# One change to a convolution and mixture-of-experts kernel: output stores of four evictions, other landing times in the list that orders the engines, and two GpSimd steps moved into that list

## The chip, the cores and the metric

The kernel runs on one core of a Trainium2 chip. The metric is the time of one execution on the device in microseconds (us). Three runs of the kernel before took 307.57, 302.77 and 307.64 us; their median is 307.57. The engines are TensorE (PE, with its weight loads as PEld), VectorE (DVE), ScalarE (ACT), GpSimd (POOL) and SyncE (SP), which issues all transfers (DMA) here.

## The reference

```python
def _attn_ref(x, weight_gen):            # x [8, 3584, 192], weight_gen [8, 3584, 8 heads, 7 taps]
    w = softmax(weight_gen, axis=-1)     # per position and head, 1e-9 added to the sum
    x_pad = concat([zeros(6 rows), x])   # causal: position s sees x[s-6 .. s]
    return einsum('bshk,bskhg->bshg', w, unfolded(x_pad))      # 24 channels per head

def _moe_ref(x, phi, w1, w2):            # x [28672, 192], phi [192, 32 slots]
    logits = x @ phi
    d = softmax(logits, axis=0)          # over all 28672 tokens, 1e-9 added to the sum
    slot_input = (d.T @ x).reshape(8 experts, 4 slots, 192)
    slot_out[e] = relu(slot_input[e] @ w1[e]) @ w2[e]          # 192 -> 1024 -> 192
    c = softmax(logits, axis=1)          # over the 32 slots
    return c @ slot_out
```

A position-dependent causal convolution of 7 taps feeds a mixture of experts, whose dispatch weights are normalised over all tokens. So nothing of the output can be computed before the last token has been convolved.

## The kernel before

**Tiles.** The 8 sequences are cut into 1,104 blocks of 26 positions; four blocks make a group (276 groups), two groups a pair (138), four pairs a block of the program's order (35, the last of two pairs), eight pairs a unit of the softmax over tokens (17, and a last one of two pairs). A chunk of taps serves eight groups, that is one block of the order; there are 35 chunks, the last one half as long.

**Stage 1, convolution (to about 221 us).** For each chunk the taps are loaded (`loadw`, L160) and pass through `tap_top` (DVE, the maximum over the taps, L171), `tap_sub` (POOL, L175), `tap_exp` (ACT, L179), `tap_sum` (three POOL steps, L188 to L190, or one on DVE), `tap_inv` (DVE, a reciprocal, L194), `tap_mul` (POOL, which writes the weights on the diagonals of `wide`, L202) and `tap_turn` (DVE, a transposition into one of three `band` buffers, L206). `taps` has three buffers too, `wide` only one. `conv` (PE, L230) multiplies bands with the rows of x, which `loadx` (L156) brings into five places of `big`; ACT copies the result to `tm` (L236); PE transposes it (L250), ACT copies that to `cm` (L257). In every second block follow, for the unit before, the scores (`logits`, PE, L281), their maximum (`top`, DVE, `mx` and `mq`, L288 and L290), a small product that gathers the maxima (`newmax`, PE, L306, and `nm`, DVE, L310), the exponentials `dd` (ACT, L318), their transposition `dt` (DVE, L327) and, one block on, the weighted sum (`dispatch`, PE, L346), which DVE adds to `accS` (L354).

**What sets the order.** In stage 1 each step is entered in a list by `op(engine, cost, reads, writes, function, ..., late, due)`. `late` is what passes after the step until its result can be used; the loads alone have one of some size. `model` goes through the list with these costs, keeps the entered order of PE and SP, picks for DVE, ACT and POOL the step with the least slack among those that can start, and yields a start for each step; the steps are written out in the order of these starts (L685). On the chip each engine runs its instructions strictly in that order and waits where an operand is missing. The numbers of the list aren't used on the chip in any other way.

**Stage 2, the experts (to about 244 us).** It is written by hand. `selO4` lies in the memory of `phi_sb`, which the scores read, and `si` in that of `fold`, which the POOL sums of the taps use; so both can be written only when those are done with. Two PE products pick the accumulators by even and odd slots (`pst`, L704 to L706), DVE copies them into the zeroed `si` (L707), `hidden` (L742) and `outputs` (L763) are the two layers. The weights `w2` are loaded into places of `big` that x no longer needs; `pace` and `mark` (L412) make each of these loads wait for a tiny POOL copy.

**Stage 3, the output (to the end).** Each piece of the output is two PE results of up to 468 columns in two PSUM banks (`rows`, L818), an eviction into `big` (`leave`, L823: DVE for each third one, from the second on, and ACT for the others) and a store (`store`, L830). `big` serves as a ring of 16 evictions. An item (0, h) is the first 128 channels of step h of 16, an item (1, h) the last 64 channels of two steps; each has two evictions, but the first one has three. Between the evictions stand the softmax steps over the slots for later steps of the output (`soft`, L85 to L99) and the transpositions `cT` (`turn`, L404).

## Time and profile before

| | |
|---|---|
| median of three runs | 307.57 us (302.77 to 307.64) |
| profiled execution | 305.91 us, span of its instructions 304.1 us |
| mean granted TensorE clock | 0.954 |
| busy PE, DVE, ACT, POOL | 263.5, 197.2, 189.6, 146.6 us |
| loads of taps | 34 of 182 KB and one of 91 KB |
| output stores | 27, of which 18 of 884 KB, 4 of 936 KB, 3 of 468 KB, 2 of 234 KB |
| written to memory | 22.04 MB |

The profile is that of one execution. A line such as "DVE top L171 <- DMA taps<-wh" says which engine waited at which line of the kernel, and for what; "in total, times, longest" follow. The chain of waits goes back from the last instruction, at each step to what released it. In lists of instructions in order of time the first number is the start after the span's begin and the second how long the piece lasted, both in us. In a table by stretches of time the columns are the length, then the busy time (and instructions) of PE, PEld, DVE, ACT and POOL, the granted TensorE clock, the busy share of the DMA engines and GB/s.

### The profile page before, as it was taken

The numbers are of one execution on the slowest core, as the hardware profiler recorded it, in microseconds if no ns is written. First come the engines' busy times: TensorE is split into PE (matmuls) and PEld (weight loads), VectorE is DVE, ScalarE is ACT, GpSimd is POOL, SyncE is SP. The second block draws the span as 40 slices with busy tenths as digits, with TensorE's granted clock in tenths as the row PEclk, the third lists the DMA queues.
The fourth block names the chain that finished last, engine by engine and source line by source line (L and its number), as shares of the span: only waits on it lengthen the run. The fifth ranks groups of instructions, "written<-read, shape, count | busy, mean of one in ns | idle before, by whom it ended". The sixth has DMA issues, their size and how long they took to land.

```text
span 304.1 us, 15222 instructions
## 1 busy us (share of the span) xinstructions
PE 263.5 (87%) x6646; PEld 213.7 (70%) x6646; DVE 197.2 (65%) x337; ACT 189.6 (62%) x399; POOL 146.6 (48%) x254
## 2 busy tenths in 40 slices
PE   8898998999999999999999999499899887889100
PEld 8787977888897888888988889488678632233000
DVE  8867757975787867775776855554056579995200
ACT  9896676576686767677767667255521268788400
POOL 8856556746468384665565463410017526550000
PEclk9999999999999999999999999979999999779855
DMA  6768676667677667666677666626748059999994
GB/s 184 220 180 240 201 214 199 208 205 207 185 216 202 201 187 202 195 194 193 185 222 216 188 204 195 195 81 182 255 130 314 3 202 416 421 410 417 419 418 204
DMA packets 26993, 69.24 MB, mean 228 GB/s; under 512 B 5936, under 2 KB 10800, under 8 KB 26928
## 3 DMA queue, kind: packets, MB, share of 16 engines
q1 hardware_dynamic: 26928, 68.28, 69.0%
q8 instruction: 52, 0.85, 1.2%
q14 instruction: 13, 0.11, 0.1%
HBM read 46.21 MB, written 22.04 MB: 224 GB/s over the span
## 4 chain that ended last, share of the span: by engine, by line
PE 69%; DMA 9%; DVE 7%; issue 4%; ACT 3%; POOL 3%; ACTq 1%; POOLq 0%; DVEq 0%
PE cv L230 30%; PE pt L250 14%; PE acb L346 7%; PE ls L281 7%; DMA out<-big 4%; DMA taps<-wh 4%; PE po L818 3%; PE so L763 2%; PE hpb L742 2%; PE acb L306 2%; DVE big L823 1%; DVE band L206 1%; POOL taps L175 1%; ACT big L823 1%; DVE cT L404 1%
## 5 line engine op out<-in xcount | busy, mean ns | idle before, releaser
L230 PE MATMUL cv<-big,band 128*26 128x96 f32 x4416 | 112.3, 250 | 3.6 <-issue 2.6
L230 PEld LDWEIGHTS cv<-big,band 128*26 128x26 f32 x4416 | 101.5, 130 | 13.0 <-issue 8.1
L236 ACT COPY tm<-cv 128x384 f32<-128x384 f32 x138 | 66.4, 482 | 57.6 <-PE cv L230 57.4
L206 DVE STREAM_TRANSPOSE band<-wide 128x1664 f32<-128x1664 f32 (+1 forms) x37 | 65.5, 1773 | 7.8 <-POOL wide L202 7.6
L250 PE MATMUL pt<-ident,tm 122*128 122x122 f32 x414 | 50.9, 272 | 0.2 <-issue 0.2
L257 ACT COPY cm<-pt 128x416 f32<-128x416 f32 x103 | 48.1, 511 | 1.9 <-PE pt L250 0.9
L250 PEld LDWEIGHTS pt<-ident,tm 122*128 122x128 f32 x414 | 44.5, 144 | 2.6 <-issue 0.4
L202 POOL TENSOR_TENSOR wide<-exps,sum 128x364 f32<-128x364 f32 (+1 forms) x36 | 28.5, 792 | 26.5 <-DVE sum L194 18.9
L175 POOL TENSOR_TENSOR taps<-taps,top 128x364 f32<-128x364 f32 (+1 forms) x36 | 28.5, 793 | 24.3 <-DVE top L171 24.0
L818 PE MATMUL po<-cT,so 32*128 32x442 f32 (+3 forms) x256 | 33.6, 629 | 5.4 <-ACT big L823 3.4
L823 ACT COPY big<-po 128x884 f32<-128x884 f32 (+2 forms) x33 | 28.1, 893 | 7.8 <-PE po L818 6.0
L818 PEld LDWEIGHTS po<-cT,so 32*128 32x128 f32 (+1 forms) x256 | 12.1, 171 | 26.4 <-ACT big L823 18.0
L188 POOL TENSOR_TENSOR si<-exps 128x208 f32<-128x208 f32 x32 | 20.3, 635 | 21.0 <-ACT exps L179 20.6
L281 PE MATMUL ls<-cm,phi_sb 128*32 128x208 f32 x544 | 28.9, 338 | 1.5 <-issue 1.5
L171 DVE TENSOR_REDUCE top<-taps 128x52 f32<-128x364 f32 (+1 forms) x37 | 17.7, 486 | 18.4 <-DMA taps<-wh 17.7
L346 PE MATMUL acb<-tm,dt 128*32 128x193 f32 x544 | 27.5, 328 | 2.3 <-issue 1.6
L87 POOL TENSOR_TENSOR LT<-LT,rm 128x544 f32<-128x544 f32 (+1 forms) x16 | 17.9, 1120 | 16.8 <-DVE rm L85 16.8
L288 DVE TENSOR_REDUCE mx<-ls 128x1 f32<-128x416 f32 x17 | 9.9, 584 | 24.0 <-PE ls L281 24.0
L281 PEld LDWEIGHTS ls<-cm,phi_sb 128*32 128x32 f32 x544 | 17.8, 109 | 6.9 <-issue 2.7
L346 PEld LDWEIGHTS acb<-tm,dt 128*32 128x32 f32 x544 | 18.0, 110 | 6.5 <-issue 3.1
L179 ACT ACTIVATE exps<-taps 128x364 f32<-128x364 f32 (+1 forms) x37 | 17.9, 493 | 6.3 <-POOL taps L175 6.3
L99 POOL TENSOR_TENSOR LT<-LT,sm 128x544 f32<-128x544 f32 (+1 forms) x16 | 17.9, 1121 | 6.8 <-DVE sm L97 6.6
(113 smaller groups left out, 260.1 us busy)
## 6 DMA issues: line engine op xcount, KB each, us to landing
big<-xh SPq DMA_DIRECT2D x276, 96.0 KB, 3.3
out<-big SPq DMA_DIRECT2D x18, 884.0 KB, 10.5
taps<-wh SPq DMA_DIRECT2D x34, 182.0 KB, 3.7
big<-w SPq DMA_DIRECT2D x8, 768.0 KB, 4.3
w1a_sb<-w1a SPq DMA_DIRECT2D x16, 256.0 KB, 3.6
out<-big SPq DMA_DIRECT2D x4, 936.0 KB, 4.9
w1b_sb<-w1b SPq DMA_DIRECT2D x8, 256.0 KB, 3.6
out<-big SPq DMA_DIRECT2D x3, 468.0 KB, 3.0
```

The source lines that it names most:

```text
L175: eng.tensor_tensor(out=t, in0=t, in1=each(tops.pop((c, b.start)), b.stop - b.start), op=ALU.subtract)
L188: eng.tensor_tensor(out=s, in0=t[:, :, :, 0:4], in1=t[:, :, :, 4:8], op=ALU.add)
L202: eng.tensor_tensor(out=dst, in0=exps[c % NEX][:, b, :, 0:KT], in1=each(m, n), op=ALU.mult)
L206: V.transpose(bands[c % NBAND][:, b].rearrange("p b j l -> p (b j l)"), wide[:, b].rearrange("p b j -> p (b j)"))
L230: P.matmul(cv[32 * blk : 32 * blk + T, o : o + 4 * GW], bands[g // 8 % NBAND][:, g // 4 % CH, :, i], xbd[:, place(t), :, b * GW : (b + 1) ...
L236: copy(tms[u % NTM][:, pr, 1 : 2 * D + 1], cvs[p % NCV][:, 0 : 2 * D])
L250: P.transpose(pt[:, at, 0:TR], tms[u % NTM][0:TR, pr, 1 + 128 * i : 129 + 128 * i], ident[0:TR, 0:TR])
L257: copy(cms[u].rearrange("p a i b j -> p (a i b) j")[:, at : at + n], pts.pop((k, j)).rearrange("p i (b j) -> p (i b) j", j=32)[:, 0:n, 0:T])
L281: P.matmul(lp[32 * blk : 32 * blk + 32, lo:hi, par, 0:T], phi_sb[:, 2 * par + i, :], cm[:, lo:hi, 1 if i else 2 * par, blk, :], start=(i = ...
L346: P.matmul(ac[32 * q : 32 * q + 32], dt[:, g, :], tm[:, g // 2, o : o + D + 1], start=(g < 4), stop=(g + 4 >= 2 * n))
L818: P.matmul(po[dst : dst + hi - lo, at, 0 : n * T], so[32 * q : 32 * q + 32, lo:hi], cT[32 * q : 32 * q + 32, g0 : g0 + n, 0:T], start=True ...
L823: (V.tensor_copy if done[1] % 3 == 1 else A.copy)(big[:, at : at + w].rearrange("p (q c) -> p q c", c=n * T), po[:, 0 : len(qs), 0 : n * T])
```

## The change

Three things are changed. In the list, a load of taps counts as 0.45 us of SP and 5.2 us until it can be used, where it was 0.4 and 4.0; a load of x counts 2.3 and 3.8, where it was 2.0 and 3.0. These numbers stand for no instruction; they change where steps of DVE, ACT and POOL stand. Two POOL steps, the zeroing of `si` and the subtraction that makes `selO4`, which stood behind the list, become steps of it. And the output is stored in pieces of four evictions, that is two items, from the seventh store on; the first five stores stay as they were, the sixth holds one item, and the last holds one too. The softmax steps between the evictions are now taken up after each eviction, where it was after each store, and the host code that unpacks the result follows.

```diff
         for c in range(NTAP, NCH):
             if k == max(0, c - 4):
-                op(SP, 0.4, [], [("w", c % NTAP, b) for b in range(CH)], loadw, c, late=4.0)
+                op(SP, 0.45, [], [("w", c % NTAP, b) for b in range(CH)], loadw, c, late=5.2)
...
-                        op(SP, 2.0, [("z", i, h) for h in range(4)], [x_of(i)], loadx, i, late=3.0)
+                        op(SP, 2.3, [("z", i, h) for h in range(4)], [x_of(i)], loadx, i, late=3.8)
...
     op(PO, 0.3, [], tmf, drop, final)
+    op(PO, 0.45, ["fold"], ["si"], lambda: G.memset(si, 0.0))
     op(TE, 0.21 * FILL[0], [], [("cv", (PAIRS + 1) % NCV)], fill, FILL[0])
-    op(TE, 0.19 * n, cm_of(final), [("ls", 1), spare], logits, final)
+    op(TE, 0.19 * n, cm_of(final), [("ls", 1), spare, "phi"], logits, final)
+    op(PO, 0.5, ["sel4"], ["phi"], lambda: G.tensor_tensor(out=selO4, in0=sel4, in1=selE4, op=ALU.subtract))
...
     bctx = ExitStack()
-    G.tensor_tensor(out=selO4, in0=sel4, in1=selE4, op=ALU.subtract)
-    G.memset(si, 0.0)
     actx.close()
...
-    for kind, h, stores in out_order():
-        for parts in stores:
-            slot += -slot % len(parts)
-            lo = at = slot % OT * 2 * 18 * T
-            for qs in parts:
-                po = ps_o.tile([128, 2, 512], F32, tag="po", name=f"po{kind}{h}_{qs[0]}")
+    for store_of in out_order():
+        slot += -slot % len(store_of)
+        lo = at = slot % OT * 2 * 18 * T
+        for kind, h, qs in store_of:
+            po = ps_o.tile([128, 2, 512], F32, tag="po", name=f"po{kind}{h}_{qs[0]}")
...
-            store(lo, at)
-            slot += len(parts)
             while late and late[0][0] < done[1]:
                 soft(pc, *late.pop(0)[1:])
-        if kind == 0 and h + 4 < len(STEPS):
-            turn(h + 4)
+            if kind == 0 and qs[-1] == 3 and h + 4 < len(STEPS):
+                turn(h + 4)
+        store(lo, at)
+        slot += len(store_of)

 def out_order():
-    for h in range(0, len(STEPS), 4):
-        for part in ((0, h), (0, h + 1), (0, h + 2), (1, h), (0, h + 3), (1, h + 2)):
-            if part == (0, 0):
-                yield *part, (((0,),), ((1,),), ((2, 3),))
-            elif part == (0, 1):
-                yield *part, (((0, 1),), ((2, 3),))
-            else:
-                yield *part, (((0, 1), (2, 3)),)
+    items = [p for h in range(0, len(STEPS), 4)
+             for p in ((0, h), (0, h + 1), (0, h + 2), (1, h), (0, h + 3), (1, h + 2))]
+    cuts = [[(0,), (1,), (2, 3)]] + [[(0, 1), (2, 3)]] * (len(items) - 1)
+    parts = [[(*item, qs) for qs in cut] for item, cut in zip(items, cuts)]
+    for p in parts[0] + parts[1]:
+        yield [p]
+    yield parts[2]
+    for i in range(3, len(parts), 2):
+        yield sum(parts[i : i + 2], [])
```

How the list moves instructions is seen on DVE near the end of stage 1, around the taps of chunk 33 (`taps_84`; the bands 91 and 92 belong to the chunks 31 and 32, `mx` and `nm` to the scores of the unit then due). Before:

```order
L206 STREAM_TRANSPOSE band_91<-wide 128x1664
L354 SCALAR_TENSOR_TENSOR accS<-accS,al_4126,acb 128x193
L171 TENSOR_REDUCE top_0_4166<-taps_84 128x52
L194 RECIPROCAL sum_0_4146<-sum_0_4146 128x52
L206 STREAM_TRANSPOSE band_92<-wide 128x1664
L288 TENSOR_REDUCE mx_4273<-ls 128x1
L290 TENSOR_SCALAR mq<-ls,mx_4273 128x4
L194 RECIPROCAL sum_0_4236<-sum_0_4236 128x52
L310 TENSOR_REDUCE nm_4289<-acb 128x1
```

And now, on the same engine:

```order
L206 STREAM_TRANSPOSE band_91<-wide 128x1664
L354 SCALAR_TENSOR_TENSOR accS<-accS,al_4122,acb 128x193
L171 TENSOR_REDUCE top_0_4218<-taps_84 128x52
L288 TENSOR_REDUCE mx_4249<-ls 128x1
L290 TENSOR_SCALAR mq<-ls,mx_4249 128x4
L194 RECIPROCAL sum_0_4228<-sum_0_4228 128x52
L310 TENSOR_REDUCE nm_4286<-acb 128x1
L327 STREAM_TRANSPOSE dt_4301<-dd 128x512
L294 STREAM_TRANSPOSE LT<-ls 128x512
L206 STREAM_TRANSPOSE band_92<-wide 128x1664
```

The transposition of the band of chunk 32 moved from ahead of the maximum of the scores to behind `dt` and `LT`. On POOL at the same place, before (`taps_86` is chunk 32, `taps_84` chunk 33, `exps_87` chunk 32, `exps_88` chunk 33):

```order
L175 TENSOR_TENSOR taps_84<-taps_84,top_0_4166 128x364
L202 TENSOR_TENSOR wide<-exps_87,sum_0_4146 128x2x26x7
L188 TENSOR_TENSOR si<-exps_88 128x208
L189 TENSOR_TENSOR si<-si 128x52x2
L190 TENSOR_TENSOR sum_0_4236<-si 128x52
L202 TENSOR_TENSOR wide<-exps_88,sum_0_4236 128x2x26x7
L314 TENSOR_TENSOR mq<-nm_4289,q_130 128x1
```

And now, on POOL:

```order
L175 TENSOR_TENSOR taps_86<-taps_86,top_0_4124 128x364
L175 TENSOR_TENSOR taps_84<-taps_84,top_0_4218 128x364
L188 TENSOR_TENSOR si<-exps_87 128x208
L189 TENSOR_TENSOR si<-si 128x52x2
L190 TENSOR_TENSOR sum_0_4228<-si 128x52
L188 TENSOR_TENSOR si<-exps_88 128x208
L189 TENSOR_TENSOR si<-si 128x52x2
L190 TENSOR_TENSOR sum_0_4269<-si 128x52
L202 TENSOR_TENSOR wide<-exps_87,sum_0_4228 128x2x26x7
L314 TENSOR_TENSOR mq<-nm_4286,q_130 128x1
L594 MEMSET si 128x400
L202 TENSOR_TENSOR wide<-exps_88,sum_0_4269 128x2x26x7
```

The sum of chunk 32 moved behind the subtraction of chunk 33, and the zeroing of `si` (now L594) stands ahead of the last full chunk's `wide`. The stores on SP, as a difference:

```order
 L830 DMA out<-big 128x468 x2
 L830 DMA out<-big 128x936 x3
-L830 DMA out<-big 128x1872 x4
-L830 DMA out<-big 128x1768 x18
+L830 DMA out<-big 128x1872
+L830 DMA out<-big 128x3744
+L830 DMA out<-big 128x3640
+L830 DMA out<-big 128x3536 x8
+L830 DMA out<-big 128x1768
```

27 stores became 17; the loads ahead of them on SP stand as they stood.

More of the change, by code (lines that the diff above doesn't have):

```diff
@@ L835, in conv_soft_moe @@
     slot = 0
-    for kind, h, stores in out_order():
-        for parts in stores:
-            slot += -slot % len(parts)
-            lo = at = slot % OT * 2 * 18 * T
-            for qs in parts:
-                po = ps_o.tile([128, 2, 512], F32, tag="po", name=f"po{kind}{h}_{qs[0]}")
-                for i, q in enumerate(qs):
-                    if kind == 0:
-                        rows(h, q, po, i, 0, 128, 0)
-                    else:
-                        rows(h, q, po, i, 128, D, 0)
-                        rows(h + 1, q, po, i, 128, D, 64)
-                at = leave(po, STEPS[h], qs, at)
-            store(lo, at)
-            slot += len(parts)
+    for store_of in out_order():
[3 more added lines that the diff above has]
+            po = ps_o.tile([128, 2, 512], F32, tag="po", name=f"po{kind}{h}_{qs[0]}")
+            for i, q in enumerate(qs):
+                if kind == 0:
+                    rows(h, q, po, i, 0, 128, 0)
+                else:
+                    rows(h, q, po, i, 128, D, 0)
+                    rows(h + 1, q, po, i, 128, D, 64)
+            at = leave(po, STEPS[h], qs, at)
             while late and late[0][0] < done[1]:
                 soft(pc, *late.pop(0)[1:])
-        if kind == 0 and h + 4 < len(STEPS):
-            turn(h + 4)
+            if kind == 0 and qs[-1] == 3 and h + 4 < len(STEPS):
+                turn(h + 4)
+        store(lo, at)
+        slot += len(store_of)
 def out_order():
-    for h in range(0, len(STEPS), 4):
-        for part in ((0, h), (0, h + 1), (0, h + 2), (1, h), (0, h + 3), (1, h + 2)):
-            if part == (0, 0):
-                yield *part, (((0,),), ((1,),), ((2, 3),))
-            elif part == (0, 1):
-                yield *part, (((0, 1),), ((2, 3),))
-            else:
-                yield *part, (((0, 1), (2, 3)),)
+    items = [p for h in range(0, len(STEPS), 4)
[7 more added lines that the diff above has]
+        yield sum(parts[i : i + 2], [])
 def _unpack(flat):
@@ L876, in _unpack @@
     at = 0
-    for kind, h, stores in out_order():
-        n = STEPS[h]
-        for parts in stores:
-            qs = sum(parts, ())
-            w = 128 * len(qs) * n * T
-            a = flat[at : at + w].reshape(128, len(qs), n, T)
-            at += w
+    for store_of in out_order():
+        ws = [len(qs) * STEPS[h] * T for _, h, qs in store_of]
+        a = flat[at : at + 128 * sum(ws)].reshape(128, sum(ws))
+        at += a.size
+        for w, (kind, h, qs) in zip(ws, store_of):
+            n = STEPS[h]
+            b, a = a[:, 0:w].reshape(128, len(qs), n, T), a[:, w:]
             q = slice(qs[0], qs[-1] + 1)
@@ L886, in _unpack @@
             if kind == 0:
-                t[0:128, q, g] = a
+                t[0:128, q, g] = b
             else:
-                t[128:D, q, g] = a[0:64]
-                t[128:D, q, step(h + 1)[0] : sum(step(h + 1))] = a[64:128]
+                t[128:D, q, g] = b[0:64]
+                t[128:D, q, step(h + 1)[0] : sum(step(h + 1))] = b[64:128]
     t = t.transpose(2, 1, 3, 0).reshape(B, NB * T, D)
```

## The prediction

> **What bounds the kernel now.** I read the page first, then the busy time by stage, then the chain of waits in order of time, then the transfers of the last stage.
>
> ```profile
> span 304.1 us, 15222 instructions
> PE 69%; DMA 9%; DVE 7%; issue 4%; ACT 3%; POOL 3%; ACTq 1%; POOLq 0%; DVEq 0%
> ```
>
> The profiled execution took 305.91 us, so 1.8 us lie outside its span of 304.1. It is 1.7 us below the median of the three runs, 307.57, and 3.1 above the lowest, 302.77. The chain that ended last runs mostly through TensorE and at its end through the output transfers. Two stages of it, the convolution and the output, with the columns PE, PEld, DVE, ACT, POOL, granted clock, DMA share, GB/s:
>
> ```profile
> 13.50:221.00 207.50, 196.96 (x5744) 174.19 (x5747) 138.71 (x221) 139.15 (x317) 108.54 (x192) 0.99 0.68 199
> ...
> 244.50:304.10 59.60, 33.59 (x256) 12.13 (x256) 33.64 (x49) 32.99 (x47) 15.38 (x14) 0.80 0.91 371
> ```
>
> In the convolution PE is busy 196.96 of 207.5 us: 10.5 us of idle time are all that a better order there can win. In the output the DMA engines are the bound. The chain shows the one large break of the convolution:
>
> ```profile
> 183.01 2.18 PE cv L230 x96
> ...
> 186.29 5.17 DMA taps<-wh
> 191.49 0.55 DVE top L171
> 192.10 0.82 POOL taps L175
> 192.93 0.79 POOL wide L202
> 193.74 1.91 DVE band L206
> 195.65 0.49 DVE mx L288
> 196.88 1.56 PE pt L250 x12
> 198.45 3.46 PE cv L230 x96
> ```
>
> A load of taps, chunk 33, is issued at 186.29 and lands 5.17 us later. DVE stands at its `top` and can do nothing behind it. Behind it stand the reciprocal and the `band` transposition of chunk 32, which waits for POOL's `wide`, which stands behind `taps` of chunk 33. Only then comes `mx`, the maximum of the scores, and PE's small product of the maxima (L306) waits for that:
>
> ```profile
> PE acb L306 <- DVE mq L290: 4.2, 2, 3.8
> 198.00:200.00 2.00, 2.00 (x47) 1.69 (x48) 2.00 (x3) 0.64 (x3) 0.28 (x1) 0.50 0.10 33
> DMA to landing us min/median/max: 2.3/3.7/5.2
> ```
> ```profile
> 191.21 1.50 PE L230 MATMUL cv<-big,band 128*26 128x96 f32 x64
> 194.80 0.28 POOL L190 TENSOR_TENSOR sum<-si 128x52 f32<-128x52 f32 x1
> 196.30 0.47 DVE L194 RECIPROCAL sum<-sum 128x52 f32<-128x52 f32 x1
> 197.82 0.71 DVE L327 STREAM_TRANSPOSE dt<-dd 128x512 f32<-128x512 f32 x1 [0.49 <-ACT dd L318]
> ```
>
> 3.8 us in one wait, and afterwards the granted clock is 0.50, so that 96 matmuls took 3.46 us where the group before took 2.18: another 1.3. The third row, over the 35 loads of taps, says that 5.2 is the worst landing and 3.7 the median; the last four rows are used below.
>
> **The change part by part.** *The list's new landing times.* They remove no instruction; they move some. In the new order `mx` stands right behind `top` of chunk 33, and the band of chunk 32 after the maxima. Put the same late load into it: `top` ends at 192.04, `mx` and `mq` at about 192.9, and PE is busy with two pairs after the scores until 191.21 + 1.50 = 192.71. So 3.6 of the 3.8 us go, and the lower clock with them: 3.6 + 1.3 = 4.9, and I take -4.9 us. What is late next is the weighted sum, one block on: it needs `nm`, ACT's `dd` and `dt`, and in the new order `nm` stands behind the reciprocal of chunk 32, whose POOL sum now stands behind `taps` of chunk 33. In the trace the sum that follows `taps` of chunk 33 on POOL (there chunk 33's own) ended at 195.08, with a `wide` of 0.8 us between them that now comes later: 194.3. From the reciprocal's start to the end of `dt` were 198.53 - 196.30 = 2.2 us: 196.5. PE comes to the product a transposition and three pairs after the maxima: 192.9 + 1.56 + 2.18 = 196.6. It just fits, in the worst landing of this trace. The bands get less lead too, as the transposition of chunk 32 moves from ahead of `mx` to behind `dt`. The cover is thin; its loss is a rival below. The bounds of this part are 0 (the wait only changes its place) and -10.5 (all idle time); I am near the middle since only this one break is large and of this kind.
>
> The granted-clock row decides 1.3 of the 4.9 us: a wait of 3.8 was followed by 0.50, and no wait of 2 or 3 us in this stage shows where that begins. The Trainium skill ("TensorE: Matmul & The Clock Gate", "What's actually happening") puts the limit at an idle window of about 3.4 us; by it a rest of the wait of, say, 3 us would cost no clock, and the term would be -(0.8 + 1.3) = -2.1 us; if the loss of clock went in proportion to the wait, it would be -(0.8 + 0.3) = -1.1.
>
> *The two POOL steps.*
>
> ```profile
> 228.36 0.41 PE L704 MATMUL pst<-selE,accS 128*128 128x32 f32 x2
> 228.50 0.45 POOL L689 TENSOR_TENSOR phi_sb<-sel,selE 128x128 f32<-128x128 f32 x1
> 228.89 0.44 POOL L690 MEMSET si<- 128x400 f32 x1
> 229.01 0.35 PE L705 MATMUL pst<-phi_sb,accS 128*96 128x32 f32 x2 [0.24 <-POOL phi_sb L689]
> 229.63 0.19 DVE L707 COPY si<-pst 128x32 f32<-128x32 f32 x1 [1.33 <-PE pst L706]
> 229.88 1.96 PE L742 MATMUL hpb<-w1a_sb,si 128*32 128x128 f32 x64
> ```
>
> L705 waits 0.24 us for the subtraction. With both steps earlier, L705 follows L704 at about 228.7 and the experts begin 0.3 us sooner; the copy L707, at 229.63, also had the memset's end (229.33) close before it and loses it. I take -0.3 (between 0 and the 0.65 from 228.36 to 229.01). In their new places both cost 0.45 and 0.44 us of POOL: the subtraction between the last scores and the accumulator's mark, where POOL is idle, the memset ahead of the band of chunk 33, which has slack of microseconds; were that gone, 0.44.
>
> *The stores.* 27 become 17: ten endings fewer, but the first store of four can't be issued until four evictions are done. Windows of the output, then the issues of the first and the seventh store, the evictions that complete the new stores, and DVE's reciprocal:
>
> ```profile
> 246.00:250.00 4.00, 3.67 (x30) 1.11 (x28) 3.32 (x6) 4.00 (x7) 0.28 (x1) 1.00 0.76 289
> 250.00:254.00 4.00, 2.76 (x32) 0.74 (x24) 4.00 (x8) 2.75 (x5) 2.41 (x3) 1.00 1.04 420
> 290.00:299.00 9.00, 0.00 (x0) 0.00 (x0) 0.00 (x0) 0.00 (x0) 0.00 (x0) 0.50 1.01 419
> ```
> ```profile
> 246.23 0.35 SPq L830 DMA_DIRECT2D out<-big  x1
> 252.74 0.33 SPq L830 DMA_DIRECT2D out<-big  x1
> 253.60 1.12 DVE L823 COPY big<-po 128x936 f32<-128x936 f32 x1
> 254.64 0.25 DVE L97 RECIPROCAL sm<-sm 128x17 f32<-128x17 f32 x1
> 257.32 0.90 ACT L823 COPY big<-po 128x884 f32<-128x884 f32 x1
> 260.52 1.67 ACT L823 COPY big<-po 128x884 f32<-128x884 f32 x2
> ```
>
> Up to and with the sixth store, which stays as it was, 2.88 MB are to be written (128 partitions x 5,616 columns x 4 bytes). The windows give 289 x 4 + 420 x 4 = 2.84 MB by 254.0, so its data end at 254.1. In the old order the seventh store has been issued by then (at 252.74). In the new one it waits for the eviction that ends at 253.60 + 1.12 = 254.72, and the reciprocal of 0.25 us now stands ahead of that: 254.97. The first packet comes 0.8 us after an issue: the first store is issued at 246.23, and the next row shows nothing moved before 247.
>
> ```profile
> DMA packets 0, 0.00 MB, mean 0 GB/s; under 512 B 0, under 2 KB 0, under 8 KB 0
> ```
>
> So the DMA engines stand idle from 254.1 to 255.8: +1.7 us, all of it on the path, since they are busy from there to the end. The next stores don't open a gap: 1.92 MB last to 260.4, and four more evictions are done at 257.32 + 0.90 = 258.2; again 1.86 MB to 264.8, against 260.52 + 1.67 = 262.2. Against it stand the endings. Two neighbouring windows of 1 us, 253 to 254 and 254 to 255, without and with the end of a store (16 small packets):
>
> ```profile
> DMA packets 59, 0.44 MB, mean 442 GB/s; under 512 B 0, under 2 KB 0, under 8 KB 59
> DMA packets 68, 0.39 MB, mean 389 GB/s; under 512 B 16, under 2 KB 16, under 8 KB 68
> ```
>
> An old store of two evictions (128 x 1,768 x 4 = 905,216 bytes) takes 2.16 us at the mean of 419 GB/s and 2.05 at 442: 0.11 us for an ending, and ten fewer save 1.1 us. No row has a store of four evictions, so it is bounded: 0 if the loss goes with the bytes, 2.7 if all 22.04 MB moved at 442. I take 1.1, the two windows' own.
>
> The Trainium skill ("DMA: Bandwidth & Descriptors", "Measured") has 341 GB/s for a transfer of 1 MB and 425 for 16 MB, and asks for 1 MiB or more. By an estimate of 380 for the double size, the paired stores' 20 MB would take 6 us less than at 341, and the sum would be near 296.4 (301.3 + 1.1 - 6). The rows disagree: stores of 0.9 MB move at 419 GB/s here, since they queue behind one another.
>
> *Sum:* 305.91 - 4.9 - 0.3 + 1.7 - 1.1 = 301.3 us.
>
> **Rivals.** *B, the wait only moves.* PE still waits about as long at another place, because 10.5 us of idle time come from many small things and a later list has as much in-order coupling. For it: DVE's waits for taps come to 17.7 us in ten times, and only one of them reached PE strongly, so which one does is partly luck. 305.91 - 0.3 + 1.7 - 1.1 = 306.2.
>
> ```profile
> DVE top L171 <- DMA taps<-wh: 17.7, 10, 4.5
> PE acb L346 <- DVE dt L327: 0.6, 1, 0.6
> ```
>
> *C, slower.* The chain from `top` of the next chunk through POOL's sum, `nm`, `dd` and `dt` to the weighted sum becomes the bound in each pair of blocks. It decides from the point at which taps land later than about 0.5 us after the scores end (in the worked case they landed 0.2 after it). Its price is the row above, 0.6 us, the wait of this kind that the trace has once, in each of 17 pairs: 10.2 us, 301.3 + 10.2 = 311.5. Against it: the median landing is 1.5 us shorter than the one worked here.
>
> *D, the stores give more.* The first gap is hidden by quicker evictions and the whole output moves at 442 GB/s: 301.3 - 1.7 - (2.7 - 1.1) = 298.0. For it speaks the window at 442, against it that every eviction up to the tenth has its old place. The Trainium skill's rule on transfer size points the same way.
>
> That the change doesn't do what it says is no case: the order shows 17 stores and the two steps in their new places.
>
> **How the numbers follow.** Forecast 0.52, B 0.25, C 0.10, D 0.13. The time is that of the likeliest, 301.3; its own range is 299 to 303.5, from the bounds of the endings and from what is left of the wait. To hold 8 in 10 the range takes B and most of D with it: 298.3 to 307. A measurement of this kernel can't tell about 2% from no change (its three runs differ by 1.6%); 2% of 307.57 is 6.15 us, so faster means below 301.4. The forecast lies on that line, and against the lowest run, 302.77, which can't have had the whole break, it would be 0.5%. So I count 0.22 of the forecast's 0.52 and all of D as faster, 0.35; 0.30 and B as within, 0.55; C as slower, 0.10.
>
> **What would show it.** Right: no wait of PE for `mq` over 1 us and no clock of 0.5 before 221; the experts' first matmul (L742) about 1.2 us after L704's start (1.5 now), and no wait of L705; a hole of 1 to 2 us in the output's transfers ahead of the first store of four; then over 420 GB/s. Wrong: PE waiting for `dt` or `band` in most pairs of blocks (C), the same idle time elsewhere (B), no hole (D), or 419 GB/s as before (the endings were free).

## The result and the profile after

| | before | after |
|---|---|---|
| median of the runs of the first comparison | 307.16 us (302.77 to 312.04, 22 runs) | 303.33 us (301.31 to 307.46, 22 runs) |
| profiled execution | 305.91 us | 302.56 us |
| granted TensorE clock, mean | 0.954 | 0.971 |
| start of L704, end of stage 1 | 228.36 us | 225.65 us |
| first output store issued | 246.23 us | 242.76 us |
| first store to the end of the span | 57.87 us | 58.04 us |

The ratio of after to before is 0.994, 95% interval 0.991 to 0.997: the change makes the kernel faster, but by less than 2%, so it counts as the same. The ratio compares only those runs of a kernel that lie near its own fastest one (the profiled execution of the kernel before isn't one of them), so a kernel of which few runs were made and none was quick looks slower by it than by its median; the medians of all runs therefore stand beside it, and here they differ by 3.83 us or 1.2%. In a later comparison (after_again, below) the ratio was 0.986, 0.979 to 0.993, and the medians differed by 4.7 us. The two intervals overlap only between 0.991 and 0.993.

The forecast was 301.3 us, that is 2.0% under the median of the runs then shown. The median came 2.0 us later. It lies in the range that was given.

The page of the changed kernel begins its chain of waits like this:

```profile
span 300.8 us, 15202 instructions
PE 69%; DVE 8%; issue 6%; DMA 6%; POOL 3%; ACT 2%; ACTq 1%; POOLq 0%; SPq 0%
```

The share of "issue" has grown from 4% to 6%, that of DMA has fallen from 9% to 6%: the loads of taps, 4.2% of the chain before, are gone from it. The waits of TensorE in the convolution, from 13.5 to 221 us, for the changed kernel, with the total, the number of times and the longest:

```profile
PE cv L230 <- issue: 5.2, 10, 1.0
PE acb L346 <- issue: 1.5, 2, 1.2
PE acb L306 <- DVE mq L290: 0.9, 2, 0.5
PE cv L230 <- DVE band L206: 0.9, 1, 0.9
PE ls L281 <- issue: 0.6, 2, 0.3
```

The one wait of 3.8 us for `mq` has become two of at most 0.5. The same view of the kernel before shows what has grown instead:

```profile
PE cv L230 <- issue: 2.6, 5, 0.9
PE acb L346 <- issue: 1.6, 3, 0.9
PE ls L281 <- issue: 1.5, 3, 0.7
PE pt L250 <- issue: 0.2, 1, 0.2
```

Together the waits listed as issue, in which TensorE waited for nothing that the profile shows, were 5.9 us before and are 7.3 now. The stretches of the changed kernel (columns as in the prediction):

```profile
13.50:221.00 207.50, 197.73 (x5763) 174.47 (x5755) 141.65 (x228) 140.66 (x320) 109.56 (x197) 1.00 0.68 199
242.50:246.50 4.00, 3.67 (x30) 1.11 (x28) 3.31 (x6) 4.00 (x7) 0.31 (x1) 1.00 0.75 287
246.50:250.00 3.50, 2.48 (x32) 0.74 (x24) 3.50 (x7) 2.25 (x5) 2.17 (x2) 1.00 1.04 423
250.00:254.00 4.00, 2.97 (x22) 1.09 (x16) 3.90 (x7) 3.33 (x6) 2.62 (x3) 1.00 0.62 256
254.00:262.00 8.00, 6.11 (x54) 1.99 (x54) 7.85 (x14) 6.55 (x10) 4.53 (x5) 1.00 1.02 432
270.00:280.00 10.00, 7.28 (x68) 2.48 (x64) 4.34 (x5) 6.07 (x8) 0.17 (x1) 1.00 1.01 428
280.00:290.00 10.00, 1.13 (x18) 0.24 (x16) 2.06 (x2) 3.39 (x4) 0.00 (x0) 0.68 1.01 430
```

The granted clock is 1.00 through the convolution. In the output the row from 250 to 254 stands out: the DMA engines are busy for 0.62 of it. From 254 on they move 428 to 432 GB/s in these rows, where the kernel before moved 415 and 414:

```profile
254.00:262.00 8.00, 5.93 (x44) 2.37 (x44) 7.91 (x14) 6.61 (x11) 5.20 (x5) 1.00 1.01 415
270.00:280.00 10.00, 9.22 (x86) 3.45 (x80) 7.73 (x10) 8.41 (x12) 1.20 (x2) 1.00 1.01 414
```

The end of stage 1 in the changed kernel, instructions in order of time:

```profile
222.17 0.46 POOL L597 TENSOR_TENSOR phi_sb<-sel,selE 128x128 f32<-128x128 f32 x1 [1.20 <-PE cv L281]
225.65 0.41 PE L704 MATMUL pst<-selE,accS 128*128 128x32 f32 x2
225.89 0.33 PE L705 MATMUL pst<-phi_sb,accS 128*96 128x32 f32 x2
226.44 0.19 DVE L707 COPY si<-pst 128x32 f32<-128x32 f32 x1 [0.85 <-PE pst L706]
226.70 1.52 PE L742 MATMUL hpb<-w1a_sb,si 128*32 128x128 f32 x48
```

The subtraction has long been done, L705 follows L704 without a wait, and from L704 to the experts' first matmul (L742) pass 1.05 us where 1.52 passed before.

### The profile page after: what moved, and what is told of

It is laid out like the page before. It is cut to its first block, busy times and chain, and to the rows that moved or that the text cites. A ratio compares the mean times of both kernels' runs of the same rounds, so it can differ in the third digit from the quotient of the medians.

```text
span 300.8 us, 15202 instructions
## 1 busy us (share of the span) xinstructions
PE 260.9 (87%) x6646; PEld 211.3 (70%) x6646; DVE 198.8 (66%) x337; ACT 190.3 (63%) x399; POOL 146.5 (49%) x254
## 4 chain that ended last, share of the span: by engine, by line
PE 69%; DVE 8%; issue 6%; DMA 6%; POOL 3%; ACT 2%; ACTq 1%; POOLq 0%; SPq 0%
PE cv L230 31%; PE pt L250 14%; PE acb L346 8%; PE ls L281 8%; DMA out<-big 5%; PE so L763 2%; PE hpb L742 2%; DVE big L823 2%; PE acb L306 2%; DVE cT L404 1%; ACT big L823 1%; DVE big L362 1%; DVE rm L85 1%; DMA big<-xh 1%; POOL LT L87 1%
## 5 line engine op out<-in xcount | busy, mean ns | idle before, releaser
L818 PE MATMUL po<-cT,so 32*128 32x442 f32 (+3 forms) x256 | 32.1, 571 | 10.2 <-ACT big L823 5.5
L818 PEld LDWEIGHTS po<-cT,so 32*128 32x128 f32 (+1 forms) x256 | 10.7, 156 | 31.2 <-ACT big L823 19.0
L281 PE MATMUL ls<-cm,phi_sb 128*32 128x208 f32 x544 | 27.9, 338 | 0.6 <-issue 0.6
L346 PEld LDWEIGHTS acb<-tm,dt 128*32 128x32 f32 x544 | 19.3, 110 | 4.8 <-issue 2.7
L194 DVE RECIPROCAL sum<-sum 128x52 f32<-128x52 f32 (+1 forms) x37 | 16.5, 445 | 8.7 <-POOL sum L190 8.4
L281 PEld LDWEIGHTS ls<-cm,phi_sb 128*32 128x32 f32 x544 | 17.0, 109 | 6.1 <-issue 1.4
```

The costliest lines, as they stand in the source:

```text
L281: P.matmul(lp[32 * blk : 32 * blk + 32, lo:hi, par, 0:T], phi_sb[:, 2 * par + i, :], cm[:, lo:hi, 1 if i else 2 * par, blk, :], start=(i = ...
L346: P.matmul(ac[32 * q : 32 * q + 32], dt[:, g, :], tm[:, g // 2, o : o + D + 1], start=(g < 4), stop=(g + 4 >= 2 * n))
L818: P.matmul(po[dst : dst + hi - lo, at, 0 : n * T], so[32 * q : 32 * q + 32, lo:hi], cT[32 * q : 32 * q + 32, g0 : g0 + n, 0:T], start=True ...
```

## The experiments

The edits are against the kernel before, where nothing else is said. Times are medians in us, with the number of runs; "before" is the kernel before on the same chip.

| run | median (runs) | before | ratio, 95% interval |
|---|---|---|---|
| e1_list | 304.09 (12) | 307.64 (23) | 0.994, 0.989 to 0.999 |
| e2_pool | 306.99 (6) | 307.64 | 1.010, 1.003 to 1.017 |
| e3_stores | 307.11 (6) | 307.64 | 1.011, 1.003 to 1.019 |
| e4_nohole | 302.25 (12) | 307.64 | 0.990, 0.985 to 0.995 |
| e5_taps | 305.28 (12) | 305.23 (23) | 0.999, 0.994 to 1.004 |
| e6_x | 305.36 (12) | 305.23 | 0.993, 0.987 to 0.999 |
| e7_later | 301.66 (6) | 305.23 | 0.984, 0.976 to 0.992 |
| e8_early | 306.23 (12) | 306.38 (17) | 1.001, 0.997 to 1.004 |
| e9_early_nohole | 302.58 (6) | 306.38 | 0.988, 0.982 to 0.995 |
| e7_again | 302.43 (6) | 306.38 | 0.988, 0.982 to 0.994 |
| after_again | 301.69 (6) | 306.38 | 0.986, 0.979 to 0.993 |
| e10_lead | 305.95 (12) | 308.03 (23) | 1.002, 0.997 to 1.007 |
| e11_lead_nohole | 306.94 (12) | 308.03 | 1.003, 0.998 to 1.009 |

### One part alone

e1_list is the list's new landing times alone.

```diff
-                op(SP, 0.4, ..., loadw, c, late=4.0)
+                op(SP, 0.45, ..., loadw, c, late=5.2)
...
-                        op(SP, 2.0, ..., loadx, i, late=3.0)
+                        op(SP, 2.3, ..., loadx, i, late=3.8)
```

> The kernel before with the four new numbers of the list alone. Theory 1 (the prediction's): the late taps in front of the maximum are a regular cost, and the new order removes 4.9 us of it; the time is 4 to 5 us (1.3 to 1.6%) under the kernel before. Theory 2: the long wait of the profiled execution is one of many that come and go; the new order only makes them rarer, and the fastest executions of both kernels differ by less than 1.5 us (0.5%). Theory 3: the list gives nothing, and the gain is in the two POOL steps and the stores; same as the kernel before.

The median fell by 3.55 us, where the whole change brought 3.83, and the ratio is that of the whole change, 0.994, which is about 1.9 us. In the profiled execution L704 started at 226.28, the longest wait for `mq` was 0.4 us, and the clock stayed at 1.00.

e2_pool is the two POOL steps alone.

```diff
+    op(PO, 0.45, ["fold"], ["si"], lambda: G.memset(si, 0.0))
...
+    op(PO, 0.5, ["sel4"], ["phi"], lambda: G.tensor_tensor(out=selO4, in0=sel4, in1=selE4, ...))
...
-    G.tensor_tensor(out=selO4, in0=sel4, in1=selE4, op=ALU.subtract)
-    G.memset(si, 0.0)
```

> The kernel before with the two POOL steps moved alone; order of the loads and stores as before. By the two traces L704 to L742 takes 1.52 us before and 1.05 after, and L742 to the first store 16.35 and 16.06: all theories say 0.5 to 0.8 us less (0.2 to 0.25%). If the steps on GpSimd delay something in the convolution, it is nothing or slower.

From L704 to L742 passed 1.05 us (228.90 to 229.95), as in the changed kernel: the term is -0.47 us. A break of 4.0 us for `mq` was there as before. The median lies 0.65 us lower; that the ratio lies above 1 all the same has the reason given with the first result, so that neither shows what the steps are worth.

e3_stores is the stores of four alone.

```diff
-            elif part == (0, 1):
-                yield *part, (((0, 1),), ((2, 3),))
-            else:
-                yield *part, (((0, 1), (2, 3)),)
...
+    yield parts[2]
+    for i in range(3, len(parts), 2):
+        yield sum(parts[i : i + 2], [])
```

> The kernel before with the stores of four evictions alone. From the first store to the end 57.9 us before and 58.0 in the changed kernel: a hole of 1.6 us in front of the first large store, and 428 instead of 418 GB/s behind it. So 0 to +0.5 us against the kernel before; the prediction's sum says +0.6. If the larger stores are worth something of their own, it is 1 us less.

e4_nohole is the whole change, but three items more have a store each, so that the first store of four comes later (18 stores instead of 17):

```diff
-    yield parts[2]
-    for i in range(3, len(parts), 2):
+    for p in parts[2:6]:
+        yield p
+    for i in range(6, len(parts), 2):
```

> The changed kernel, but the third to sixth item are still stored as two evictions each, and stores of four begin with the seventh item: the hole in front of the first large store should be gone, the faster transfers behind it stay. 1.3 to 1.7 us less than the changed kernel, that is 3.2 to 3.6 us (1.1%) under the kernel before in like runs; if the hole is hidden by something else, the same as the changed kernel (0.994).

The stretches of the output, of e3_stores:

```profile
254.00:262.00 8.00, 7.60 (x44) 3.48 (x48) 7.75 (x12) 7.04 (x11) 4.89 (x5) 0.57 0.81 341
270.00:280.00 10.00, 8.49 (x74) 2.71 (x66) 6.79 (x10) 7.10 (x11) 1.60 (x2) 0.93 1.01 425
```

The stores alone make the hole (a DMA share of 0.81 in 8 us is 1.5 us of rest) and the quicker transfer after it; from the first store to the end it is 58.16 us, 0.3 more than in the profiled execution before. Of e4_nohole:

```profile
248.00:252.00 4.00, 3.51 (x22) 1.28 (x16) 3.89 (x7) 3.33 (x6) 2.61 (x3) 0.72 1.01 417
252.00:256.00 4.00, 4.00 (x32) 1.62 (x28) 3.85 (x7) 4.00 (x6) 1.97 (x3) 0.50 0.93 379
256.00:264.00 8.00, 6.60 (x60) 2.31 (x48) 7.84 (x14) 6.07 (x11) 5.42 (x6) 0.96 1.01 423
```

There the hole is gone from this place, with a small one of 0.4 us from 252 on (379 GB/s in 4 us at a rate of some 420; the granted clock was 0.50 there), and from the first store to the end pass 56.93 us, 1.1 less than in the changed kernel. The other kernels without the hole show 56.8 to 57.1 (e7_later, e7_again, e9_early_nohole, e11_lead_nohole).

### Which number of the list

e5_taps has the new numbers for taps alone, e6_x those for x alone, and e7_later still later ones for both (6.4 and 4.6) in the version without the hole.

```diff
-                op(SP, 0.45, ..., loadw, c, late=5.2)
+                op(SP, 0.45, ..., loadw, c, late=6.4)
...
-                        op(SP, 2.3, ..., loadx, i, late=3.8)
+                        op(SP, 2.3, ..., loadx, i, late=4.6)
```

> The kernel before with the taps' two numbers of the list alone (0.45 and 5.2); x as before (2.0 and 3.0). Theory 1: it is the taps that stand in the way between the maximum, nm and dt; in the kernel before a top stands between mx and dt in 14 of 17 units, here in 2, so all of the list's gain should be here, 3 to 4 us under the median of the kernel before, and no wait of TensorE for mq or dt over 1 us. Rival: it is the whole list, x included, that spaces the steps; then about half, 1.5 to 2 us.

> The kernel before with the two numbers for x alone (2.3 and 3.8); taps as before (0.4 and 4.0). Theory 1 by its simple form: no gain, since the taps are what lands late. Its refined form: what counts is whether a top stands between mx and dt; the numbers for x alone leave that in 6 of 17 units where it was 14, so more than half of the gain, 2 to 3 us, should come from them too.

> The changed kernel with stores of two until the sixth item (as in the run without the hole), and landing times later still in the list: 6.4 for taps, 4.6 for x. If later is better, under 302.2 us. If there is a best value, because top comes back in front of dt (in 14 of 17 units again) and the bands lose their lead, 2 us or more above the run without the hole, and waits of TensorE for mq, dt or band of 1 us and more come back.

My idea was that the units count in whose order on DVE a `top` stands between the maxima and `dt`. Counted again over all 18 units, they are 12 before, 4 in e5, 5 in e6, 5 in the changed kernel and 13 in e7, not the counts that those expectations give. With these counts the idea falls: e7_later has the most of them and was the quickest run, e5 and e6 have no more than the changed kernel and didn't lower the median. With one number alone a wait for `mq` of some size was left, 2.6 us in e5 and 1.6 in e6; with both none over 0.5 was left in e1_list. But L704 started at 225.57 and 226.16 in e5 and e6, no later than with both numbers, no clock was lost, and by the ratio e6 (0.993) is as good as the whole change. A further execution with both numbers had a wait of 4.0 us (a_look2, below). So which of the numbers matters is not shown.

The wait of 2.6 us matters for another step. The product in e5_taps that waited, and then the stretch behind it:

```profile
62.18 0.36 PE L306 MATMUL acb<-mq,sel 128*128 128x5 f32 x2 [2.56 <-DVE mq L290]
```
```profile
62.00:65.00 3.00, 2.82 (x74) 2.69 (x78) 2.71 (x6) 1.69 (x4) 2.84 (x5) 1.00 0.88 242
```

It cost no clock. Nor did a longer one, of 2.83 us, in another execution of the kernel before (b_look2, below):

```profile
204.23 0.36 PE L306 MATMUL acb<-mq,sel 128*128 128x5 f32 x2 [2.83 <-DVE mq L290]
204.23:205.23 1.00, 1.00 (x10) 1.00 (x11) 0.65 (x3) 0.35 (x1) 0.69 (x1) 1.00 0.76 231
```

### Loads one block earlier

If taps come late, an earlier load should do as well as a list that counts them later. e8_early keeps the old list and gives taps a fourth buffer, in a part of `LT` that is not used before the last scores:

```diff
-        for c in range(NTAP, NCH):
-            if k == max(0, c - 4):
+        for c in range(3, NCH):
+            if k == max(0, c - 5):
```

> The kernel before, with its old list numbers, old POOL steps and old stores, but with a fourth buffer for taps (in a part of the array LT that is not used before the last scores) so that each load of taps is issued one block of the order, about 6 us, earlier. Theory (the one large break comes from taps that land later than the list counts, so the list's later landing times and an earlier load are two cures of one thing): DVE's waits for taps fall from 17.7 us to under 6, no wait of PE for mq is over 1 us, no granted clock of 0.5 stands before the end of stage 1, the first selection of the accumulators (L704) starts at 224.5 to 226 where the kernel before has 228.7, and the median is 2.5 to 4 us below the median of the kernel before (ratio 0.987 to 0.992). Rival (the new order itself is better, landing has little to do with it): a wait for mq of 3 us or more stays, L704 starts at 228 or later, ratio 0.997 to 1.003.

e9_early_nohole is e4_nohole with the same earlier loads. e7_again and after_again are e7_later and the changed kernel once more, on the same chip.

> The changed kernel with the single-item stores kept for four items longer (as in the run without the hole) and with the same earlier loads of taps. Theory: with the loads early, the new landing times have nothing left to cure, and the two gains do not add: as the run without the hole, whose profiled execution took 299.5 and whose median was 302.3; ratio against the kernel before 0.985 to 0.992. Rival (the two add, since some waits for taps and bands of 2.7 us were left in that run): 1.5 to 2.5 us below it, ratio 0.978 to 0.985.

> A repeat of the kernel with later landing times still (6.4 for taps, 4.6 for x) and without the hole, beside the changed kernel on one chip. Theory (its first result, ratio 0.984, is real): 2 to 4 us below the changed kernel. Rival (its few runs of the first time were lucky ones, and it gains only what leaving out the hole gains): 0.5 to 1.5 us below the changed kernel.

> The changed kernel once more, on the chip of the three others. Theory: a ratio of 0.99 to 0.996 to the kernel before, as its first comparison gave (0.994), since the break of 3.8 to 5.3 us is in most executions of the kernel before but not in all. Rival (the first comparison understated it, and the full forecast of 2% holds): 0.978 to 0.984.

e8_early did nothing for the median. DVE's waits for taps fell to 10.1 us and none of PE for `mq` was left, but PE waited 1.96 us at the same product for POOL's `taps`, which stands behind `top`, and 1.5 for `dt`. The product, and the stretch around it:

```profile
48.27 0.47 PE L308 MATMUL acb<-mq,sel 128*128 128x5 f32 x2 [1.96 <-POOL taps L177]
```
```profile
48.00:52.00 4.00, 3.73 (x42) 3.45 (x46) 3.57 (x7) 1.53 (x3) 3.61 (x9) 0.57 0.57 157
```

The shorter wait cost clock where the longer ones cost none, and L704 (there L706) started at 229.48. The test wasn't a clean one: the list saw the loads early and put their use early too. After_again agrees with the first comparison in sign and lies, at 0.986, between the two forecasts; beside it on one chip the versions without the hole were no quicker: 302.6 and 302.4 against 301.7. The 1.1 us of the hole, which the traces show, don't show in the medians of six runs each.

### How often the break comes

b_look is one more execution of the kernel before, beside e5 to e7; b_look2, b_look3, a_look2 and a_look3 are further single executions of the two kernels as they are.

> The kernel before itself, another execution. The three profiles so far with its list (before, the one with the POOL steps, the one with the stores) each have one wait of TensorE for mq, of 3.8, 4.0 and 4.3 us, in different places. If the break belongs to the order, here is one too, of 3 to 5 us, at whatever place a load of taps comes late; if it was chance, there is none and the time is under 303 us.

> The kernel before, one more profiled execution. Theory (the break is in every execution, at a place that varies): one wait of PE of 3.5 to 5.5 us for mq, a granted clock of 0.5 for 3.3 or 6.7 us behind it, 1.6 to 3.2 us lost by that, L704 at 228 to 229.5, waits listed as issue 5 to 6 us. Rival (quick executions lack it): no wait over 2 us, L704 before 226.

> As the other look at the kernel before. Theory: a break of 3.5 to 5.5 us with low clock, L704 at 228 to 229.5. Rival: none, L704 before 226.

> The changed kernel, one more profiled execution. Theory: no wait of PE over 2 us and no clock under 1 before L704, L704 at 224.5 to 226; waits listed as issue 7 to 9 us, that is 1.5 us or more above those of the kernel before. Rival (those waits only vary): 4.5 to 6.5 us.

> As the other look at the changed kernel. Theory: no break, L704 at 224.5 to 226, issue 7 to 9 us. Rival: issue 4.5 to 6.5 us.

The profiled executions with the old list and with the new one, all with three buffers of taps, in us; the waits are those of TensorE from 13.5 to 221, and "clock" is the busy time of TensorE in each microsecond times what was missing of the granted clock there:

| | L704 | longest wait for `mq` | all for `mq` | clock | issue |
|---|---|---|---|---|---|
| before | 228.36 | 3.8 | 3.8 | 1.7 | 5.9 |
| b_look | 229.21 | 5.3 | 5.7 | 2.7 | 5.4 |
| b_look2 | 234.61 | 4.3 | 8.2 | 1.7 | 6.3 |
| b_look3 | 235.62 | 3.4 | 3.7 | 3.2 | 8.5 |
| e2_pool | 228.90 | 4.0 | 4.0 | 3.2 | 5.3 |
| e3_stores | 228.24 | 4.3 | 4.3 | 3.1 | 5.7 |
| *mean, old list* | 230.8 | | 5.0 | 2.6 | 6.2 |
| after | 225.65 | 0.5 | 0.9 | 0 | 7.3 |
| after_again | 224.80 | 0.5 | 0.9 | 0 | 7.1 |
| a_look2 | 230.20 | 4.0 | 4.3 | 2.8 | 6.3 |
| a_look3 | 226.57 | 0.5 | 1.4 | 0 | 7.6 |
| e1_list | 226.28 | 0.4 | 0.8 | 0 | 8.9 |
| e4_nohole | 223.90 | 0.5 | 1.4 | 0 | 6.1 |
| *mean, new list* | 226.2 | | 1.6 | 0.5 | 7.2 |

With the old list the break is in six executions of six, with the new one in one of six. So my theory that the new list has no break fell with a_look2. Nor is the place with the old list any place: in five of the six the break stands at the same scores, near 50 us. The one of the profiled execution before, at 196 us, is the rarer; b_look2 alone has a wait there too, the 2.83 us above, beside its break near 50.

Near 50 us the traces show what the new list does. The old order has `top`, a band and then `mx` on DVE (the rows of b_look below, with a load issued 0.9 us after the scores of the unit, L281, had begun). The new order has `mx` first and this `top` behind it. In a_look2 the same load was as late, issued 1.0 us after the same scores had begun, and the product of the maxima (L306) didn't wait:

```profile
43.60 1.57 PE L281 MATMUL ls<-cm,phi_sb 128*32 128x208 f32 x27
44.62 0.39 SPq L160 DMA_DIRECT2D taps<-wh  x1
46.08 0.59 DVE L288 TENSOR_REDUCE mx<-ls 128x1 f32<-128x416 f32 x1 [0.62 <-PE ls L281]
47.28 0.39 PE L306 MATMUL acb<-mq,sel 128*128 128x5 f32 x2
47.69 0.53 DVE L171 TENSOR_REDUCE top<-taps 128x52 f32<-128x364 f32 x1 [0.76 <-DMA taps<-wh]
```

In the profiled execution after the change that load was issued as the same scores began (43.08 and 43.12), with no wait behind it either. So there the new order, and not an earlier load, took the break away.

The break of a_look2 stands elsewhere, at 89 us. The instructions of SP, DVE and PE around it, and the stretch behind it:

```profile
76.68 5.01 SPq L156 DMA_DIRECT2D big<-xh  x8
81.79 0.37 SPq L160 DMA_DIRECT2D taps<-wh  x1
81.97 1.59 PE L281 MATMUL ls<-cm,phi_sb 128*32 128x208 f32 x32
85.70 0.53 DVE L171 TENSOR_REDUCE top<-taps 128x52 f32<-128x364 f32 x1 [5.60 <-DMA taps<-wh]
86.14 1.90 DVE L206 STREAM_TRANSPOSE band<-wide 128x1664 f32<-128x1664 f32 x1
87.97 0.55 DVE L288 TENSOR_REDUCE mx<-ls 128x1 f32<-128x416 f32 x1
88.92 0.56 PE L306 MATMUL acb<-mq,sel 128*128 128x5 f32 x2 [4.05 <-DVE mq L290]
```
```profile
89.00:92.00 3.00, 3.00 (x18) 2.69 (x21) 2.62 (x5) 1.62 (x3) 2.70 (x5) 0.50 0.98 243
```

At this place the new order too has `top`, then a band, and only then `mx`. And this load was not slow: from its issue at 81.79 to the start of `top` at 85.70 it is 3.9 us, where the median landing of that run is 3.7. It was issued late, 0.2 us before the scores of the unit began (L281), behind eight loads of x that kept SP for 5 us. In the profiled execution after the change the same load left 4.8 us before the same scores (77.08 and 81.92). In the other four executions with the new list it left 4.1 to 4.8 us before them, and DVE's wait for it was 2.5 us at most. In a_look2 SP had fallen behind step by step: the three loads of taps up to this one were issued 2.6, 3.1 and 4.7 us later than in the profiled execution after the change, and the second of them held SP for 1.67 us (0.38 there). Why SP was slower in that execution no run here shows. The break of b_look is of the same kind:

```profile
43.81 0.38 SPq L160 DMA_DIRECT2D taps<-wh  x1
47.92 0.53 DVE L171 TENSOR_REDUCE top<-taps 128x52 f32<-128x364 f32 x1 [5.52 <-DMA taps<-wh]
51.15 0.56 PE L306 MATMUL acb<-mq,sel 128*128 128x5 f32 x2 [5.33 <-DVE mq L290]
```

From issue to use these seven breaks took 5.2 (before), 4.1 (b_look), 3.3 (b_look2), 5.0 (b_look3), 2.9 (e2_pool), 3.1 (e3_stores) and 3.9 us (a_look2). Only two of them are loads of the slow kind that the prediction spoke of. In six of the seven the load was issued between 0.4 us before and 1.9 us after the scores of the unit began (L281); in the profiled execution before it was 3.5 us before.

b_look2 and b_look3 took 312.2 and 312.9 us, on a chip where another run of the kernel before took 305.1. Up to L704, against the mean of the other four executions with the old list, b_look2 has 3.5 us more in waits for DVE, 1.4 more in issue waits and 0.9 more of busy time; b_look3 has 4.4 more in issue waits, 3.3 more of busy time and 1.0 less in waits for DVE. That is 5.8 of the 5.9 us, and 6.7 of the 6.9, by which they end stage 1 later; the break of b_look3 is no larger than the others'. Why the issue waits and the busy time were larger stays open.

### More lead for the loads

e10_lead is e8_early with the list told to count the landing 6 us later, so that the use keeps its place and only the lead in time grows. e11_lead_nohole does this to the version without the hole.

```diff
-                op(SP, 0.4, ..., loadw, c, late=4.0)
+                op(SP, 0.4, ..., loadw, c, late=10.0)
```

> The kernel before with four buffers of taps, each load issued one block earlier, and the list counting 10.0 us until it can be used (4.0 before, plus the 6 us of a block), so that the use stays at about its old place and the load has about 6 us more lead. Old POOL steps, old stores, old number for x. Theory (breaks come from loads that SP issues too late for their use): DVE waits for taps fall from 17.7 us to under 5, no wait of PE for mq over 1 us, no clock of 0.5 before L704, L704 at 223.5 to 226, median 3 to 5 us under the kernel before. Rival (something else holds DVE or PE at that place): a break of 2 us or more stays, L704 at 227.5 or later, median within 1.5 us.

> The changed kernel without the hole, with the same early loads, and the list counting 10.8 us for taps (x as in the changed kernel). Theory: no break in any profiled execution, L704 at 223 to 225, profiled execution 298 to 300.5, median 300 to 302, ratio 0.978 to 0.987. Rival (a break is rare enough with the changed list already): no better than the version without the hole, median 302 to 303.

In both no wait of DVE for taps is listed in the convolution, and none of PE for `mq`. That part of the theory stands, in one execution each: with loads that are issued earlier for the same use the break didn't come. But the time did not follow. L704 (there L706) started at 228.08 and 228.19, where 226 and 225 were the latest forecast; e11's profiled execution took 305.18 us, and both ratios lie at 1.00. The wait has a new place. The longest waits of TensorE in the convolution, of e10_lead:

```profile
PE cv L232 <- DVE band L208: 6.2, 2, 5.2
```

and of e11_lead_nohole:

```profile
PE cv L232 <- DVE band L208: 6.7, 3, 5.2
```

The wait of 5.2 us is one, at 29.6 and 29.9 us: the first loads can't be issued earlier than the start, the list counts 10 us for them all the same, and I take this to be why the first bands stand late. By the table's measure the wait and the clock behind it cost e10 5.2 and 1.5 us, more than the 3.8 and 1.7 of the break in the profiled execution before. A version that counts the long landing only from the sixth chunk on wasn't tried, so neither the cause of this wait nor the worth of the lead alone is shown.

## Why the prediction was right or wrong

**The break and its clock: right in kind.** That there would be "no wait of PE for `mq` over 1 us and no clock of 0.5 before 221" held in the profiled execution and in five of six with the new list. Means over the six and six executions: the waits for `mq` fell by 3.3 us (forecast 3.6), the loss by clock by 2.1 (forecast 1.3).

**The list's term: the step that failed.** The term was "-4.9 us", with the break taken whole and nothing put against it. In the profiled pair L704 came 2.71 us earlier. There 2.9 us of waits for `mq` went, and 1.7 of clock, but the waits listed as issue grew by 1.4, and another 0.5 is spread. Over the six and six L704 came 4.6 us earlier on the mean, near -4.9, but that mean holds the two long executions of one kernel and the other's one execution with a break; of the four executions on each side without b_look2, b_look3, a_look2 and a_look3 the means are 228.7 and 225.2, -3.5. The list alone (e1_list) brought 3.55 us by the medians and about 1.9 by the ratio. So the term was too large by 0.3 to 3.0 us, depending on the executions taken. Whether the growth of the issue waits belongs to the list can't be said: 5.3 to 8.5 us with the old, 6.1 to 8.9 with the new.

**What the number was held against.** The sum gave -4.6 us against the profiled execution, 1.5%. I then measured it against a median that lay 1.7 us higher and called the result 2.0%. The profiled pair differs by 3.35 us, 1.1%, the medians by 3.83. The prediction had said of the lowest run shown, 302.77, that it "can't have had the whole break", and that against it the gain would be 0.5%; the ratio gave 0.6%. Whether the shortest executions of the kernel before lack the break is not shown: the shortest profiled execution with the old list took 305.81 us (e2_pool).

**Why the load was late.** The prediction read the break as a landing of 5.17 us, "in the worst landing of this trace", and judged the new order by such a landing. That is the exception: in six of the seven breaks SP issued the load no earlier than 0.4 us before the scores, and five of them stand near 50 us, a place that the prediction didn't work out. That a `top` ahead of `mx` turns a late load into a wait of PE, and that the new order takes it away, was right, and a_look2 shows it near 50 us; that the new order does so there too was luck as far as the working goes. Where the new order keeps `top` and a band ahead of `mx`, an ordinary landing was enough, once the load was issued late: the cover that I called thin did go once. Why SP issues late in some executions no run here shows.

**The rule on the clock.** I weighed a limit of 3.4 us of idle time (the Trainium skill, "TensorE: Matmul & The Clock Gate", "What's actually happening"), by which a rest of the wait of 3 us would have cost no clock. The runs say otherwise: a wait of 1.96 us (e8_early) cost clock, one of 2.23 (e9_early_nohole) did, and those of 2.56 us (e5_taps) and 2.83 (b_look2) didn't. Read in steps of 0.25 us, the low stretches last 3.4 us (before, e8, e9) or 6.8 (e2, e3). The same section of the Trainium skill says that the window runs freely and is 3.4 us long; with that the lengths of the low stretches agree, while the need of a whole idle window is not borne out.

**POOL steps.** Forecast -0.3, measured -0.47 in both pairs of traces; no wait of L705. The experts' own part, L742 to the first store, took 0.3 us less in the changed kernel (16.06 against 16.35), which the prediction didn't have. It isn't tied to the change: in e2_pool it took 16.52 and in three further executions of the kernel before 16.07 to 16.38.

**The hole.** Forecast 1.7 us, measured 1.6: 256 GB/s in 4 us at a rate of 423 is 2.4 us of transfer. The transfers of the changed kernel around it, and then the issue that ends it:

```profile
250.00:250.50 0.50, 0.32 (x8) 0.00 (x0) 0.50 (x3) 0.50 (x1) 0.21 (x1) 1.00 0.94 389
250.50:251.00 0.50, 0.19 (x2) 0.19 (x4) 0.50 (x1) 0.26 (x1) 0.50 (x1) 1.00 0.27 105
251.00:252.00 1.00, 1.00 (x8) 0.41 (x6) 1.00 (x2) 0.57 (x2) 1.00 (x2) 1.00 0.00 0
252.00:252.50 0.50, 0.43 (x4) 0.00 (x0) 0.40 (x2) 0.50 (x2) 0.46 (x1) 1.00 1.13 479
```
```profile
251.43 0.33 SPq L830 DMA_DIRECT2D out<-big  x1
```

The first store of four was issued 8.7 us after the first store, as worked out (254.97 less 246.23). Undone alone (e4_nohole) the hole gives back 1.1 us, near 1.6 less the small hole of 0.4 and one more ending.

**The endings.** Forecast -1.1. In the four stretches from 254 to 290 (8, 8, 10 and 10 us) the rates went from 415, 416, 414 and 418 GB/s to 432, 417, 428 and 430, on the mean from 416 to 427; for the 19.2 MB behind the sixth store this is 46.1 against 44.9 us, -1.2. From first store to end, though, it is +0.17 where the sum had +0.6. The Trainium skill's table ("DMA: Bandwidth & Descriptors", "Measured") is of loads into SBUF that GpSimd issues; taken for these stores, as the prediction did, it would have made the sum 296.4, which these rates don't bear out: 1.8 MB moved at 427 GB/s where 0.9 MB had moved at 416.

**The rivals.** B, that the wait only moves, is in part what happened: in a_look2 to a break at another place, on the mean to some more issue waits; its 306.2 was too long by 2.9 us. C, a wait for `dt` in each pair, didn't come: no such wait is listed in the changed kernel. D fell with the hole, which is there.

## What to carry to other kernels

A break seen in one execution is one draw: before it goes into a sum, look at a few more profiled executions, and ask at which place it stood in each, for what came late may be the issue of a load and not its landing. Where loads of several kinds share one in-order queue, compare the time of issue with the time of use before a landing time is put into a planner; a number there that is too large for the first loads costs a wait at the start. A larger store saves its endings only if the first one isn't held back by the evictions that it gathers: measure the hole and the endings separately.

## What I had not expected of the hardware

The granted clock fell after a wait of 1.96 us and not after one of 2.83, and it stayed low for about 3.4 us or twice that, so the length of a wait alone didn't decide what it cost. Waits of TensorE listed as issue come to 5 to 9 us in the convolution, in 11 to 16 pieces of up to 1.7 us (the twelve executions of the table). For two of the longest, at 77.37 us (after, 1.17 us) and 27.28 us (before, 0.94 us), the queue of instructions had moved a packet of 16 KB in the 1 us from 74 and from 24, some 2 us before the wait began. The twelve traces show that this is no chance: each of the 154 such waits began 0.8 to 2.8 us after a packet of that queue, where the packets lie 4.6 us apart on the mean and fewer than half of all moments lie so behind one. So these waits go with the loading of instructions. Whether TensorE stood still for want of instructions is not shown, and no run here changed the loading.
